# Sliding-window attention beside a gated feed-forward: attention kept transposed, its weights spread through DRAM, the down projection behind the next projections

## The chip, the cores and the metric

One core of a Trainium2 chip runs the kernel. Its engines work side by side, each on its own queue of instructions in order: TensorE (PE: matmuls, with weight loads PEld), VectorE (DVE), ScalarE (ACT), GpSimd (POOL) and SyncE (SP, which here only issues DMAs). Data move between DRAM, the SBUF (128 partitions) and the PSUM banks that TensorE writes. The metric is the time of one execution on the device, in microseconds (us); lower is better.

## The reference

The input is 2048 tokens of width 640 (bf16). A layer norm without learned scale feeds two branches whose sum is added to the input:

```python
def _A_ref(x, wqkv, wo):                 # D = 640, H = 32 heads, Dh = 20
    W, dil = 8, 2
    qkv = (x @ wqkv).reshape(B, S, 3, H, Dh).transpose(2, 0, 3, 1, 4)
    q, k, v = qkv[0], qkv[1], qkv[2]
    idx = pos[:, None] - off[None, :]    # off = 0, 2, ..., 14
    mask = idx >= 0
    ...
    logits = jnp.einsum("bhsd,bhswd->bhsw", q, kg) * scale
    logits = jnp.where(mask[None, None, :, :], logits, -1e9)
    attn = _softmax(logits, axis=-1)
    o = jnp.einsum("bhsw,bhswd->bhsd", attn, vg)
    return o.transpose(0, 2, 1, 3).reshape(B, S, D) @ wo

def _B_ref(x, w_gate, w_up, w_down):     # F = 1536
    return ((x @ w_gate) * (x @ w_up)) @ w_down

xn = _layernorm(x, axis=-1)
return x + _A_ref(xn, A_wqkv, A_wo) + _B_ref(xn, B_w_gate, B_w_up, B_w_down)
```

So each token attends, per head, to eight tokens: itself and those 2, 4, ... 14 positions back.

## The kernel before

**Tiling.** The 2048 tokens are 16 tiles of 128 (index t), grouped into four chunks of 512 (index c). The width 640 is five groups of 128 (KT), the inner width 1536 twelve (FT). `xnT` holds a chunk's normalized input transposed: width on partitions, tokens along the free axis.

**Order.** The kernel does not issue instructions as its loops run. Each piece of work is a `Step` with an engine, a cost, dependencies (`deps`) and an order (`after`); `Plan.order` (L56) simulates the engines, takes at each point the ready step with the least slack, and the instructions are issued in the order that results. `pe_main` (L367) chains PE's steps into a fixed sequence and gives them six PSUM banks in turn (`ring`); only the logits are slipped in between (`urgent`). A step's `margin` is time that the planner adds to a wait. The DMAs on SP are a queue in order too: a DMA that waits holds those behind it.

**Per chunk.** Normalization (`ln`, L334) on DVE for the first eight tiles, on ACT and POOL for the rest; transposes (`transposes`, L379) on PE for chunk 0, by DMA from SP for the others. `qk` (L454) projects q and k transposed: output width on partitions (so that the four partitions jl of a head and the five groups hold its 20 elements), 512 tokens free, five banks each of five matmuls. Their weights are read with a stride of five columns. ACT copies the banks to `q` and `k`; `k` has 14 extra tokens in front (`halo`, L442). `vproj` (L488) projects values the other way: 128 tokens on partitions, two banks of 320 columns a tile; ACT copies them with the heads innermost to `v_t`, and POOL stores them to a DRAM buffer `vD`.

**Attention.** `products` (L559) multiplies q with k shifted by each of the eight offsets, two offsets an instruction, on DVE. `fold` (L538) adds the five groups: in chunks 1 to 3 down to one term, written over the parts of `q` and `k` no longer needed; in chunk 0 only to three (FIRST = 1, LEFT). `logits` (L583) sums over the four partitions of a head with a matrix of ones, `Ek`, on PE: four matmuls side by side, each giving 32 heads on their own 32 partitions; chunk 0 does this once for each of its three terms and lets PSUM add. Half a chunk, n, fills one bank: partition = offset pair and head, free = tokens. The first half's bank gets the mask. ACT copies the bank to `L`, and a DMA transpose on SP turns it to `LT`: tokens on partitions, offsets and heads free. `softmax` (L627) then works on 2 x 8 x 32 values a partition: maximum by three pairwise steps, subtract, exponential on ACT, sum by three steps, reciprocal, scaling to the weights `a`.

**Values.** `load_v8` (L670) loads, for a tile, the eight shifted value rows of each token from `vD`: 1280 KB, three buffers. `av` (L698) multiplies them with the weights (5120 elements a partition), adds the eight offsets in three steps to `o` (tokens on partitions), and a DMA transpose on SP makes `oT`.

**Feed-forward.** `glu` (L742): for each of 12 groups, five matmuls of 512 columns for gate and five for up; ACT copies both banks, DVE multiplies them to `hT`. `down` (L800) adds, for each tile, twelve matmuls with `wd` over `hT` and five with `wo` over `oT` in one bank, in two column halves; ACT copies, and POOL adds the result onto the output in DRAM, which was seeded with the input (`seed`, L783). The last two tiles are added to the input on DVE and stored by SP.

**Sequence on PE.** At the start, tile by tile while input arrives: transposes and values of chunk 0; then q, k of chunk 0 and the fourth tile's values, q, k and values of chunk 1. Then per chunk c: gate and up of c, down of c (with the normalization of chunk c+2 between its tiles, `between`, L914), and q, k, values of c+2. The value weights are loaded first, on ACT's queue; q's and k's follow on SP's, then gate, up, and, behind value loads, down's and the output's.

Of the kernel before, what the change touches and what calls it, by code (L numbers as in the profile page):

```python
# [14 lines left out]
class Step:  # L15


    __slots__ = ("eng", "cost", "deps", "fn", "late", "succ", "idx", "start", "end", "left", "occ", "urgent", "after", "floor", "margin", "kb")

    def __init__(self, eng, cost, fn, deps, occ=None, after=()):  # L20
        self.eng, self.cost, self.fn = eng, cost, fn
        self.after = [d for d in after if d is not None]
        self.deps = [d for d in deps if d is not None] + self.after
        self.occ = cost if occ is None else occ
        self.succ = []
        self.urgent = False
        self.floor = 0.0
        self.margin = 0.0
        self.kb = 0


class Plan:
# [3 lines left out]
    RAW = 0.116  # L36
    INORDER = ("DVE", "PE", "ACT")
# [4 lines left out]
    def add(self, eng, cost, fn, deps=(), occ=None, after=(), kb=0):  # L42
        s = Step(eng, cost, fn, deps, occ, after)
        s.kb = kb
        s.idx = len(self.steps)
        self.steps.append(s)
        return s
# [8 lines left out]
    def order(self):  # L56
# [4 lines left out]
        for s in reversed(self.steps):  # L61
            s.late = min([t.late for t in s.succ], default=0.0) - s.cost
# [45 lines left out]
def kernel(  # L108
# [17 lines left out]
    H = 32  # L126
# [33 lines left out]
    negm = const.tile([P, 2, HALO], F32, name="negm")  # L160
    vD = dram.tile([HALO + S, D], BF, name="vD")
# [28 lines left out]
    WL = {}  # L190

# [5 lines left out]
    def part(n):  # L197
        src = A_wqkv[:, 2 * D + n * NS : 2 * D + (n + 1) * NS].rearrange("(i p) f -> p i f", p=P)
        return lambda: nc.scalar.dma_start(out=wv[:, :, n * NS : (n + 1) * NS], in_=src)
# [8 lines left out]
    def consts0():  # L208
        wz = new("wz", [P, CS], BF, "gs", 5)
        nc.vector.memset(wz[:], 0.0)  # L210
        hold(wv)()
# [10 lines left out]
    def consts_m():  # L222
        nc.gpsimd.memset(negm[:], 0.0)
        for i in range(W):
            w = W - 1 - i
            if w:
                nc.gpsimd.memset(negm[H * (i % 4) : H * (i % 4 + 1), i // 4, 0 : DIL * w], -1e9)

    def consts_z():
        zt = new("zt", [P, D], BF, "v_t", 3)  # L230
        nc.gpsimd.memset(zt[0:HALO, :], 0.0)
        nc.gpsimd.dma_start(out=vD[0:HALO, :], in_=zt[0:HALO, :])

    wo_r = A_wo.rearrange("(h j) d -> j h d", h=H, j=Dh)

    def wo_load():
        for jl in range(JL):
            src = wo_r[jl : jl + 1, :, :]
            src = bass.AP(tensor=src.tensor, offset=src.offset, ap=[[Dh * D, H], [JL * D, KT], [1, D]])
            nc.sync.dma_start(out=wo[jl * H : (jl + 1) * H, :, :], in_=src)  # L240

    C0 = add("POOL", 0.6, consts0)
    WV = [add("ACT", 4.6, part(0), [C0], occ=0.45)]
    WV.append(add("ACT", 5.6, part(1), occ=0.45, after=[WV[0]]))
    X[3] = add("ACT", 5.0, load_x(3, nc.scalar), occ=0.45, after=[WV[1]])
    TB = add("ACT", 1.6, table, after=[X[3]])
    CZ = add("POOL", 3.0, consts_z, [C0], occ=1.2)
# [63 lines left out]

    def ln_mean(t):
# [63 lines left out]
    XDMA = 4  # L376
    GP = {}

    def transposes(t):  # L379
        c, q = divmod(t, CH)  # L380

        def slot():
            if q == 0:
                new(("xnT", c), [P, KT, CS], BF, "xnT", 2)
# [27 lines left out]
        if t < CH:  # L412
# [7 lines left out]
            if t:  # L420
                behind(VE[t - 1][0], TT[t])
# [5 lines left out]
        else:  # L427
            if c == 1:
                a = TT[t] = chain[0] = add("SP", 3.0, dma, [XT[t]], occ=1.28, after=[chain[0]])
            else:  # L430
                a = TT[t] = add("SP", 2.8, dma, [XT[t], GP.get(c - 2)], occ=1.28, kb=200)
# [7 lines left out]
    Q, Kk, LL = {}, {}, {}  # L439
    HALOCP = {}  # L440

    def halo(c):  # L442
        def fn():
            k = new(("k", c), [P, KT, HALO + CS], BF, "k", 2)
            if c == 0:
                nc.vector.memset(k[:, :, 0:HALO], 0.0)
            else:
                nc.scalar.copy(k[:, :, 0:HALO], T["k", c - 1][:, :, CS : CS + HALO])
        if c == 0:
            HALOCP[c] = add("DVE", 0.1, fn)  # L450
        else:
            HALOCP[c] = add("ACT", 0.25, fn, [LL.get(2 * c - 3), *Kk[c - 1]])

    def qk(c, lo, n, rs=(0, 1)):  # L454
        for r in rs:
            for j in range(KT):
                key = ("qk", c, r, j, lo)

                def pe(i0, i1, key=key, r=r, j=j):
                    if i0 == 0:  # L460
                        new(key, [P, 512], F32, "ps", 6, psum)
                    for i in range(i0, i1):
                        nc.tensor.matmul(T[key][:, 0:n], lhsT=(wk if r else wq)[:, i, :].rearrange("p (c b) -> p c b", b=KT)[:, :, j],  # L463
                                         rhs=T["xnT", c][:, i, lo : lo + n], start=(i == 0), stop=(i == KT - 1))

                def ev(key=key, r=r, j=j):
                    if r == 0 and j == 0 and lo == 0:
                        new(("q", c), [P, KT, CS], BF, "q", 2)
                    dst = T["k", c][:, j, HALO + lo : HALO + lo + n] if r else T["q", c][:, j, lo : lo + n]
                    nc.scalar.copy(dst, T[key][:, 0:n])  # L470

                one = n / 2400 + 0.0027
                ts = range(c * CH + lo // P, c * CH + (lo + n) // P)
                mine = [WK if r else WQ, *[TX.get(t, TT[t]) for t in ts], LL.get(2 * c - 3)]
                if c or r or j:
                    a = pe_main(KT * one, lambda pe=pe: pe(0, KT), mine + [TT[t] for t in ts])
                else:
                    pe_main(3 * one, lambda pe=pe: pe(0, 3), mine)
                    a = pe_main(2 * one, lambda pe=pe: pe(3, KT), [TT[t] for t in ts], banks=0)
                e = add("ACT", 0.16 + n / 1200, ev, [a, HALOCP[c]], occ=0.07 + n / 1200)  # L480
                ring.append(e)
                (Kk if r else Q).setdefault(c, []).append(e)

    VS = {}

    VE = {}

    def vproj(t, ns=(0, 1)):  # L488
        c, q = divmod(t, CH)
        evs = VE.setdefault(t, [])  # L490
        for n in ns:
            def pe(i0, i1, n=n):
                if i0 == 0:
                    new(("psv", t, n), [P, 512], F32, "ps", 6, psum)
                for i in range(i0, i1):
                    nc.tensor.matmul(T["psv", t, n][:, 0:NS], lhsT=T["xnT", c][:, i, q * P : (q + 1) * P],  # L496
                                     rhs=wv[:, i, n * NS : (n + 1) * NS], start=(i == 0), stop=(i == KT - 1))

            def ev(n=n):
                if n == 0:  # L500
                    new(("v_t", t), [P, D], BF, "v_t", 3)
                nc.scalar.copy(  # L502
                    T["v_t", t][:].rearrange("p (j h) -> p j h", j=Dh, h=H)[:, :, n * H // 2 : (n + 1) * H // 2],
                    T["psv", t, n][:, 0:NS].rearrange("p (h j) -> p j h", h=H // 2, j=Dh),
                )

            if t < 3 and n == 0:
                pe_main(3 * 0.136, lambda pe=pe: pe(0, 3), [TX[t], WV[n]])
# [476 lines left out]
```

## Time and profile before

| | |
|---|---|
| median of 3 runs | 260.86 us (260.27 to 261.1) |
| the profiled execution | 262.23 us |
| its span, first to last instruction | 260.5 us |
| granted TensorE clock | 1.00 |
| busy, share of span: POOL, ACT | 22%, 51% |
| bytes moved by DMA | 46.54 MB, 179 GB/s |
| value loads, v<-vD | 16 of 1280 KB, 9.3 us to landing (median) |
| value stores, vD<-v_t | 16 of 160 KB, 5.1 us |
| transposes LT, oT, xnT | 8, 16, 12; 3.1, 3.6, 4.0 us |
| gate, up, down weights | 1920 KB each; 8.6, 12.6, 11.0 us |

All durations come from the one profiled execution; the span is what its trace covers, and 1.73 us lie around it. A group line of the profile reads: line of the kernel, engine, operation, output <- inputs, shapes, count | busy us in all, mean ns of one | idle time of the engine just before them and what ended it. A line of the waits reads: who <- for whom: us in total, times, longest. A line of the timeline reads: start, length, engine, line, operation, count, idle before and what ended it. Matmuls are pipelined and their ends are modelled: a single one shows 379 ns at 512 columns while they follow each other faster, so distances between starts are the better measure.

### The profile page before, as it was taken

The page shows a single profiled execution, that of the slowest core. Times are in us where ns is not written, and L with a number is a line of the kernel's source. Part 1 is how long each engine was busy: PE and PEld are TensorE (multiplying, and loading weights), DVE is VectorE, ACT ScalarE, POOL GpSimd, SP SyncE. Part 2 cuts the span into 40 slices and gives each one's busy share as a digit, 9 for nine tenths or more (in the row PEclk, how much of TensorE's full clock was granted, in tenths as well). Part 3 has the DMA queues.
Part 4 walks back from the last instruction along what each step waited for, and adds up shares of the span by engine and source line. Part 5 has one row for each costly group of instructions (what it writes and reads, how often), then busy time and mean ns, then how long its engine had stood idle before and what let it go on. Part 6 is the DMA issues. An engine that isn't in the chain of part 4 may idle for free.

```text
span 260.5 us, 3925 instructions
## 1 busy us (share of the span) xinstructions
PE 253.1 (97%) x1462; PEld 141.1 (54%) x1462; DVE 221.4 (85%) x308; ACT 132.2 (51%) x265; POOL 57.6 (22%) x93
## 2 busy tenths in 40 slices
PE   6999999999997999999999999999999999999895
PEld 2655555444675656544467655644457654445563
DVE  5764998899999968999999959989999887699711
ACT  3755566699821357579951255475531245283100
POOL 4650002054731201107932110200121210000110
PEclk9999999999999999999999999999999999999999
DMA  7999997999999422993339956951136849951341
GB/s 222 340 264 178 397 384 166 337 363 248 200 163 254 49 35 48 366 259 106 127 109 149 247 49 199 337 217 25 25 101 72 227 41 309 184 170 25 49 54 50
DMA packets 51507, 46.54 MB, mean 179 GB/s; under 512 B 24626, under 2 KB 49472, under 8 KB 51424
## 3 DMA queue, kind: packets, MB, share of 16 engines
q1 hardware_dynamic: 46704, 37.10, 53.1%
q0 software_dynamic: 3184, 8.05, 16.2%
q10 hardware_dynamic: 1600, 1.15, 1.4%
q8 instruction: 11, 0.18, 0.3%
q14 instruction: 8, 0.07, 0.1%
HBM read 35.39 MB, written 7.55 MB: 165 GB/s over the span
## 4 chain that ended last, share of the span: by engine, by line
PE 56%; DVE 10%; DMA 6%; issue 1%; ACT 0%; SPq 0%
PE ps L751 20%; PE ps L814 16%; PE ps L463 8%; PE ps L817 7%; DVE v L705 5%; PE ps L496 4%; DMA v<-vD 4%; DMA oT<-o 2%; DVE v L714 2%; DVE hT L767 1%; PE pl L592 1%; DVE v L718 1%; DVE o L723 0%; DVE s L639 0%; DVE d L644 0%
## 5 line engine op out<-in xcount | busy, mean ns | idle before, releaser
L751 PE MATMUL ps<-xnT,wg 128*128 128x512 bf16 x240 | 59.6, 379 | 0.0
L751 PE MATMUL ps<-xnT,wu 128*128 128x512 bf16 x240 | 59.6, 379 | 0.0
L814 PE MATMUL ps<-wd,hT 128*128 128x320 bf16 (+2 forms) x384 | 57.6, 299 | 0.9 <-DVE hT L767 0.9
L705 DVE TENSOR_TENSOR v<-v,a 128x5120 bf16<-128x5120 bf16 x16 | 45.1, 2820 | 2.5 <-DMA v<-vD 2.3
L814 PEld LDWEIGHTS <-hT 128*128 128x128 bf16 x384 | 36.9, 98 | 17.4 <-DVE hT L767 1.4
L573 DVE TENSOR_TENSOR pw<-q,k 128x2560 bf16<-128x2560 bf16 x28 | 41.0, 1486 | 5.4 <-ACT k L470 5.2
L751 PEld LDWEIGHTS <-wu 128*128 128x128 bf16 x240 | 23.5, 98 | 28.3
L751 PEld LDWEIGHTS <-wg 128*128 128x128 bf16 x240 | 23.4, 98 | 27.8 <-issue 0.2
L829 ACT COPY y<-ps 128x320 f32<-128x320 f32 x28 | 11.5, 426 | 51.1 <-PE ps L817 38.4
L756 ACT CAST us<-ps 128x512 bf16<-128x512 f32 x48 | 28.1, 586 | 13.1 <-PE ps L751 11.8
L756 ACT CAST gs<-ps 128x512 bf16<-128x512 f32 x48 | 28.2, 587 | 12.3 <-PE ps L751 12.3
L858 POOL DMA_DIRECT2D out_dram<-y x14 | 12.2, 871 | 82.2 <-ACT y L829 82.2
L817 PE MATMUL ps<-wo,oT 128*128 128x320 bf16 (+2 forms) x160 | 27.0, 299 | 1.5 <-DMA oT<-o 1.5
L544 DVE TENSOR_TENSOR pw<-pw 128x2048 bf16<-128x2048 bf16 (+1 forms) x26 | 24.4, 971 | 0.0
L496 PE MATMUL ps<-wv,xnT 128*128 128x320 bf16 x160 | 23.4, 299 | 0.4 <-ACT xnT L409 0.4
L714 DVE TENSOR_TENSOR v<-v 128x2560 bf16<-128x2560 bf16 x16 | 23.7, 1483 | 0.0
L463 PE MATMUL ps<-xnT,wq 128*128 128x512 bf16 x100 | 22.5, 380 | 0.2 <-DMA xnT<-x 0.2
L463 PE MATMUL ps<-xnT,wk 128*128 128x512 bf16 x100 | 22.3, 379 | 0.0
L517 POOL DMA_DIRECT2D vD<-v_t x16 | 9.0, 563 | 56.9 <-ACT v_t L502 56.9
L767 DVE TENSOR_TENSOR hT<-gs,us 128x512 bf16<-128x512 bf16 x48 | 19.4, 415 | 0.7 <-ACT us L756 0.7
L817 PEld LDWEIGHTS <-oT 128*128 128x128 bf16 x160 | 15.4, 98 | 8.0 <-DMA oT<-o 1.8
L496 PEld LDWEIGHTS <-xnT 128*128 128x128 bf16 x160 | 15.1, 98 | 7.7 <-issue 1.1
(71 smaller groups left out, 233.1 us busy)
## 6 DMA issues: line engine op xcount, KB each, us to landing
v<-vD SPq DMA_DIRECT2D x16, 1280.0 KB, 9.3
vD<-v_t POOLq DMA_DIRECT2D x16, 160.0 KB, 5.1
out_dram<-y POOLq DMA_DIRECT2D x14, 160.0 KB, 3.8
out_dram<-in_A_x_dram POOLq DMA_DIRECT2D x3, 640.0 KB, 4.3
wg<-in_B_w_gate_dram SPq DMA_DIRECT2D x1, 1920.0 KB, 8.6
wu<-in_B_w_up_dram SPq DMA_DIRECT2D x1, 1920.0 KB, 12.6
wd<-in_B_w_down_dram SPq DMA_DIRECT2D x1, 1920.0 KB, 11.0
x<-in_A_x_dram SPq DMA_DIRECT2D x11, 160.0 KB, 4.9
```

The lines of the kernel that those rows point to most:

```text
L463: nc.tensor.matmul(T[key][:, 0:n], lhsT=(wk if r else wq)[:, i, :].rearrange("p (c b) -> p c b", b=KT)[:, :, j], rhs=T["xnT", c][:, i, lo ...
L496: nc.tensor.matmul(T["psv", t, n][:, 0:NS], lhsT=T["xnT", c][:, i, q * P : (q + 1) * P], rhs=wv[:, i, n * NS : (n + 1) * NS], start=(i == ...
L544: nc.vector.tensor_tensor(w[:, :, lo:hi, :], w[:, :, lo:hi, :], w[:, :, a:b, :], ALU.add)
L573: nc.vector.tensor_tensor(o, qh, kh, ALU.mult)
L705: nc.vector.tensor_tensor(v[:].rearrange("p w (j h) -> p w j h", j=Dh, h=H), v[:].rearrange("p w (j h) -> p w j h", j=Dh, h=H), T["a", n][ ...
L714: nc.vector.tensor_tensor(v[:, 0:4, :], v[:, 0:4, :], v[:, 4:8, :], ALU.add)
L751: nc.tensor.matmul(ps[:], lhsT=(wu if r else wg)[:, i, f * P : (f + 1) * P], rhs=T["xnT", c][:, i, :], start=(i == 0), stop=(i == KT - 1))
L756: nc.scalar.copy(s[:], T[key][:])
L767: nc.vector.tensor_tensor(h[:], T["gs", c, f][:], T["us", c, f][:], ALU.mult)
L814: nc.tensor.matmul(ps, lhsT=T["hT", c, f][:, q * P : (q + 1) * P], rhs=wd[:, f, sl], start=(f == 0), stop=(f == FT - 1 and not wo_part))
L817: nc.tensor.matmul(ps, lhsT=T["oT", t][:, g, :], rhs=wo[:, g, sl], start=False, stop=(g == KT - 1 and f1 == FT))
L858: nc.gpsimd.dma_start(out=out_flat[t * P : (t + 1) * P, :], in_=T["y", t][:], accum_op=ALU.add)
```

## The change

**Values** are projected like q and k (`proj`, three times per chunk, and `project`): transposed, into a tile `v` with 14 extra tokens in front, two buffers. The DRAM buffer `vD`, the value stores, the eight-fold loads, `L`, `LT` and their transposes are gone. At the start it is now q that is projected tile by tile (`proj_tile`: 128-column matmuls, five output groups in two banks); its weights come first, on ACT's queue, split by rows, and those of k and v follow on SP's.

**Logits and softmax.** Chunk 0 folds to one term as well (FIRST = 3), so each half takes one pass. A bank now holds all eight offsets and 64 tokens on the free axis; the partition is the head and which quarter of the half's 256 tokens (E = 64). Eight matmuls of 256 columns fill it. `softmax` works on the bank itself: two reductions (`top`, `total`) take the place of the six pairwise steps; `d`, `m`, `s` and `a` have one buffer.

**Weights.** `store` writes the half's weights `a` to DRAM (128 KB), and `spread` loads them back with each head's row repeated on its four partitions (512 KB). `av` multiplies shifted windows of `v` with them, two instructions a tile, and adds the offsets; the last step writes `oT` itself, so its transpose is gone. `wo` is loaded in one DMA with partitions in the projections' order.

**Order.** After gate and up of chunk c, PE does q, k and values of chunk c+2 and then down of chunk c. `xnT` has three buffers. The normalization on ACT is held by the steps in LN_HOLD. The planner multiplies DVE costs by 1.03, and the logits' margin is 3 us instead of 4.

The diff, cut to its core:

```diff
+    PACE = {"DVE": 1.03, "ACT": 1.0}
...
+    LN_HOLD = ((2,1,0),(2,1,2),(2,1,4),(0,0),(0,11),(2,2,0),(2,2,1),(2,2,2))
...
-            a = GL[t] = add("ACT", 0.95, ln_mean(t), [X[t], HT.get((t // CH - 2, t % CH + 2))], occ=0.87)
+            a = GL[t] = add("ACT", 0.95, ln_mean(t), [X[t], held(LN_HOLD[t - 2 * CH])], occ=0.87)
...
+    EARLY = True
+    XB = 3 if EARLY else 2
...
+    def proj_tile(r, t, ns=(0, 1)):
+        for n in ns:
+            j0, j1 = ((0, 3), (3, KT))[n]
+            def pe(i0, i1, n=n, j0=j0, j1=j1):
+                for j in range(j0, j1):
                     for i in range(i0, i1):
+                        nc.tensor.matmul(T["psv", r, t, n][:, (j - j0) * P : (j - j0 + 1) * P], lhsT=lhs(r, i, j),
+                                         rhs=T["xnT", c][:, i, q * P : (q + 1) * P], start=(i == 0 and j == j0), stop=(i == KT - 1),
...
+    def proj(c, r, lo=0, n=CS):
+        for j in range(KT):
+            def pe(key=key, j=j):
+                for i in range(KT):
+                    nc.tensor.matmul(T[key][:, 0:n], lhsT=lhs(r, i, j),
+                                     rhs=T["xnT", c][:, i, lo : lo + n], start=(i == 0), stop=(i == KT - 1))
+            old = LL.get(2 * c - 3) if r < 2 else O16.get(CH * (c - 1) - 1)
...
+                for b in range(2):
+                    for j in range(4):
+                        nc.tensor.matmul(l[H * j : H * (j + 1), 4 * b : 4 * b + 4, :], lhsT=Ek[:],
+                                         rhs=parts[b][i][:, :, E * j : E * (j + 1)],
...
+        def top():
+            m = new(("m", n), [P, E], F32, "m", 1)
+            nc.vector.tensor_reduce(m[:], T["lps", n][:].rearrange("p w s -> p s w"), AX.X, ALU.max)
         def sub():
+            d = new(("d", n), [P, W, E], F32, "d", 1)
+            nc.vector.tensor_tensor(d[:], T["lps", n][:], T["m", n][:, None, :].to_broadcast([P, W, E]), ALU.subtract)
...
+        def total():
+            s = new(("s", n), [P, E], F32, "s", 1)
+            nc.vector.tensor_reduce(s[:], T["d", n][:].rearrange("p w s -> p s w"), AX.X, ALU.add)
...
+        def store():
+            aD = new(("aD", n), [H, 4, W * E], BF, "aD", 2, dram)
+            nc.sync.dma_start(out=aD[:].rearrange("h e f -> e h f"), in_=T["a", n][:].rearrange("p w s -> p (w s)"))
+        def spread():
+            ae = new(("aE", n), [P, 4, W, E], BF, "aE", 2)
+            src = bass.AP(tensor=src.tensor, offset=src.offset, ap=[[4 * W * E, H], [0, JL], [1, 4 * W * E]])
+            nc.sync.dma_start(out=ae[:], in_=src)
+        AS[n] = add("SP", 2.4, store, [AA[n], AE.get(n - 2)], occ=0.5, kb=128)
+        AE[n] = add("SP", 3.5, spread, [AS[n], AM.get(2 * n - 3)], occ=0.5, kb=512)
...
+        def mul(b):
+                o = T["av", t][:, :, :, b * E : (b + 1) * E]
+                w = bass.AP(tensor=w.tensor, offset=w.offset, ap=[list(w.ap[0]), [E, W], [0, KT], [1, E]])
+                v = T["v", c][:, :, q * P + b * E : q * P + b * E + E]
+                v = bass.AP(tensor=v.tensor, offset=v.offset, ap=[list(v.ap[0]), [DIL, W], *[list(x) for x in v.ap[1:]]])
+                nc.vector.tensor_tensor(o, v, w, ALU.mult)
...
-        between(c + 2, lambda q: down(c * CH + q))
-        if c + 2 < NCH:
-            halo(c + 2)
-            qk(c + 2, 0, CS)
+            if c + 2 < NCH:
+                for t in range((c + 2) * CH, (c + 3) * CH):
+                    ln(t)
+                    transposes(t)
+                project(c + 2)
             for q in range(CH):
-                vproj((c + 2) * CH + q)
+                down(c * CH + q)
```

More of the change, by code (lines that the diff above doesn't have):

```diff
@@ L447, in fn @@
             else:
-                nc.scalar.copy(k[:, :, 0:HALO], T["k", c - 1][:, :, CS : CS + HALO])
+                nc.scalar.copy(k[:, :, 0:HALO], T[PROJ[r], c - 1][:, :, CS : CS + HALO])
         if c == 0:
-            HALOCP[c] = add("DVE", 0.1, fn)
+            HALOCP[r, c] = add("POOL", 0.3, fn, after=[RS[0]])
         else:
[L452 to L461, printed above, removed]
-                    for i in range(i0, i1):
[L463 to L508, printed above, removed]
-                a = pe_main(2 * 0.136, lambda pe=pe: pe(3, KT), [TT[t]], banks=0)
-            else:
-                a = pe_main(KT * 0.136, lambda pe=pe: pe(0, KT), [TT[t], TX.get(t), WV[n]])
-            e = add("ACT", 0.425, ev, [a, VS.get(t - 3), CZ], occ=0.35)
```

320 lines of the change are left out of this document (153 added, 167 removed).

## The prediction

> **What bounds the kernel now.** First the page's busy shares, then TensorE (PE) in order of time, then who waited for whom on VectorE (DVE), last the groups by shape for prices.
>
> ```profile
> span 260.5 us, 3925 instructions
> PE 253.1 (97%) x1462; PEld 141.1 (54%) x1462; DVE 221.4 (85%) x308; ACT 132.2 (51%) x265; POOL 57.6 (22%) x93
> PE 56%; DVE 10%; DMA 6%; issue 1%; ACT 0%; SPq 0%
> ```
>
> A busy PE need not be PE at its rate, so I check it: the chain of waits has the gate and up matmuls of chunk 1 as 120 in 25.90 us, 0.216 each for 512 columns, and the 320-column ones as 12 in 1.63, 0.136 each. At these rates the timeline has PE back to back nearly from 6.54 us to the last matmul. The places where it is not are these (start, length, what; a length includes the modelled end of the last matmul, so I use counts times the rates):
>
> ```profile
> 22.36 1.52 PE L496 MATMUL ps<-wv,xnT 128*128 128x320 bf16 x10
> 24.10 5.59 PE L463 MATMUL ps<-xnT,wq 128*128 128x512 bf16 x25 [0.22 <-DMA xnT<-x]
> ...
> 77.23 1.79 PE L814 MATMUL ps<-wd,hT 128*128 128x320 bf16 x12
> 80.50 0.85 PE L817 MATMUL ps<-wo,oT 128*128 128x320 bf16 x5 [1.47 <-DMA oT<-o]
> ...
> 241.26 0.84 PE L817 MATMUL ps<-wo,oT 128*128 128x320 bf16 x5
> 242.56 0.31 PE L814 MATMUL ps<-wd,hT 128*128 128x320 bf16 x1 [0.45 <-DVE hT L767]
> 243.30 2.21 PE L814 MATMUL ps<-wd,hT 128*128 128x320 bf16 x15 [0.43 <-DVE hT L767]
> ```
>
> The gaps: 24.10 - (22.36 + 1.36) = 0.38 us (the transposed chunk 1 is late), 80.50 - (77.23 + 1.63) = 1.64 (the attention output's transpose is late for the down projection), 242.56 - (241.26 + 0.68) = 0.62 and 243.30 - (242.56 + 0.14) = 0.60 (the last products of gate and up). Together 3.24 us. PE is the bound and there is little to take from it; DVE at 85% is close behind.
>
> ```profile
> DVE m L639 <- DMA LT<-L: 7.6, 6, 1.9
> DVE pw L573 <- ACT k L470: 5.2, 1, 5.2
> DVE s L639 <- ACT d L652: 3.3, 3, 1.9
> DVE v L705 <- DMA v<-vD: 2.3, 1, 2.3
> ```
>
> These are totals, times, longest. DVE starts attention at 23.18 (after the 5.2 us wait for k) and ends it at 246.03, 222.85 us; in them it waits 7.6 + 3.3 + 2.3 + 0.7 (for up) = 13.9, so it has 208.9 us of work.
>
> ```profile
> L705 DVE TENSOR_TENSOR v<-v,a 128x5120 bf16<-128x5120 bf16 x16 | 45.1, 2820 | 2.5 <-DMA v<-vD 2.3
> L573 DVE TENSOR_TENSOR pw<-q,k 128x2560 bf16<-128x2560 bf16 x28 | 41.0, 1486 | 5.4 <-ACT k L470 5.2
> L814 PEld LDWEIGHTS <-hT 128*128 128x128 bf16 x384 | 36.9, 98 | 17.4 <-DVE hT L767 1.4 <-issue 0.5
> L463 PEld LDWEIGHTS <-wq 128*128 128x128 bf16 x100 | 11.6, 118 | 9.8 <-DMA xnT<-x 0.5 <-issue 0.2
> ```
>
> **The change on PE.** Values: 160 matmuls of 320 columns (21.8 us) become 25 of 512 per chunk, 5.4 per chunk: nothing. In chunk 0 the part done tile by tile while inputs arrive is now q, in 128-column matmuls, a new weight for each: 100 of them. The nearest row is the last tile's 12 matmuls of 128 columns in 0.67 us in the chain, 0.056 each, 5.6 against 40 x 0.136 = 5.4 for values before: +0.2. But q's weights are read with a stride of five columns and such a load takes 118 ns, not 98. Bounds: 0.056 (load hidden) and 0.118 (nothing overlaps), +0.2 to +6.4. I take 0.058, +0.4, since 98 ns loads already run at a 0.056 spacing, so a load's length isn't its spacing. The first 0.38 of a delay here is free: chunk 1 waits for its transpose anyway. So 0 on the path.
>
> The Trainium skill (TensorE: Matmul & The Clock Gate, Back-to-back issue gap) says that a stream of load and matmul pairs at 128 columns runs at about 81 ns a pair. The trace's 0.67/12 = 56 ns disagrees, for packed weights; by the page the sum would be some 2.3 us higher. This is the first rival.
>
> Logits: chunk 0 had three rounds of four concurrent 512-column matmuls per half (37.05 to 37.82, 0.77 us), the others one round (0.33), so a round is 0.22 and the fixed part 0.11. Now each half is two rounds of 256 columns. If a round is half as long: 0.33, two halves save 0.87 in all. If a round's four weight loads set it, 0.22 stays: 0.55, chunk 0 saves 0.44 and six halves lose 1.3: +0.9. I take the middle, 0.
>
> Down of chunk 0 moves behind the 16.2 us of q, k, v of chunk 2 (3 x 25 x 0.216), from 68 to about 84 us. The outputs it waited for until 80.5 are ready long before (below), and they are written by DVE itself, without the 3.6 us transpose. The 1.64 us gap goes. What is late next there: project of chunk 2 at 68 needs the chunk's normalized, transposed input some 20 us earlier than before (88.1). That work now starts at the value evictions of chunk 1 (about 35 us), where ScalarE (ACT) is 5.9 of 10 busy from 40 to 50; four tiles cost 4 x (0.74 + 0.19 + 0.84 + 0.20 + 0.93) = 11.6 us of ACT beside 24 evictions of 0.59; in the trace the same mix fitted 50 to 70 us without a PE stall. A third buffer takes away the wait for the old chunk. Without that cover, each microsecond late is one on PE.
>
> The 1.22 us at the end: DVE must hand over the last products earlier. I count 0.8 of them. Sum on PE: -1.64 - 0.8 + 0 + 0 = -2.4 us.
>
> **On DVE.** Removed per half chunk, by the groups' means: maximum tree 0.290 + 0.221 + 0.187, sum tree 0.420 + 0.287 + 0.225, 1.63 in all. Added: two reductions of 512 f32 values, not in the trace. Below, the 256-pair level, 0.420; nearest, a 512-element f32 pass, 0.69; above, twice that, 1.38 (logits' bank, strided). 16 x r - 13.0: -6.3, -2.0, +9.1; I take -2.0. Subtraction, reciprocal and scaling keep their size (subtract now reads the bank itself; 0.69 kept). Weighting the values: 2 x 1.486 for 2.820, the products being the same size, type and kind: 16 x 0.152 = +2.4. Chunk 0's sums now fold to one term on DVE: 8 x 0.686 = +5.5. Together +5.9: 214.8 us of work. It starts earlier: q is ready 1.4 us after values were, k 5.4 later, so about 19.3 instead of 23.2. Without waits DVE ends at 234.1; with all 13.9 of the old waits at 248.0. The last output is needed about 255.5 - 2.4 = 253 (the last tile's wo matmuls stand at 255.54). So DVE may idle 19 us before the end moves, which covers the +5.9; without cover it would be +5.9.
>
> The output of the last half is not late either way, but the products of gate and up are in the same line, so I keep 0.4 of the end gaps.
>
> **DMA and the queues.** Gone: 16 loads of 1280 KB (9.3 us median, 6.1 to 15.6), 17 stores, 16 output transposes, 8 logit transposes (1.19 us of SP's queue each, 3.1 to landing, the 7.6 us of DVE waits). New per half: a store of 128 KB, then, after it lands, a load of 512 KB, both on SP in order. Behind a waiting store stand the transposes for chunk c+2 and further loads. A small store at the end (160 KB) landed in 1.8 us; loads of 160 KB took 2.3 to 8.4. So the trip is 4 to some 17 us; I take 6 (store 2, load 4). DVE has the second half's products (about 10 us with folds) or two tiles of the half before (2 x 5.4) in that time.
> Values of chunk 2 overwrite those of chunk 0, so ACT's evictions at 78 wait until DVE has finished the fourth tile: 19.3 + 21 (products, folds) + 2 x 3.3 + 4 x 5.4 + 12 x 0.34 = 72.6 us. Behind a blocked ACT stand PE's banks: five groups fit, so PE stops only from about 84. That allows 11 us of slip.
> ACT loses the logits' copies (4.7 us) and gains three halo copies (0.8); POOL loses the 9.0 us of value stores. Neither sets the end. The planner's factor of 1.03 on DVE and its logits margin of 3 us for 4 change the order only: a logits group placed 1 us earlier holds PE if the folds are late, and so far PE waits for none.
>
> **Sum.** The profiled execution took 262.23 us with 1.73 around its span; the runs' median is 260.86, 1.4 lower. 260.5 - 2.4 gives a span of 258.1; taken off the median, 258.5.
>
> **Rivals.**
> 1. *q's strided weights set the pace.* If the 20 ns by which they are longer all shows, 0.076 a matmul, 7.6 us for 5.4: +2.2 - 0.38 = +1.8, giving 260.2; this is no measurable change. For: 118 against 98. Against: at 512 columns the strided ones run at 0.216 like the packed.
> By the page named above it would be 100 x 0.081 = 8.1, +2.3, so 260.7.
> 2. *The trip through DRAM (slower).* Place: between scaling and the first weighting of each half, on SP's in-order queue. In chunk 0 the new load stands behind gate, up, down and out weights, 6.6 MB at the 380 GB/s of those slices, 17 us from 21.9. If a trip takes 12 us against 8.5 of cover, 8 x 3.5 = 28 us of DVE idle; DVE ends at 262 instead of 253, +9 on the span of 258.1: about 267 for the median. It decides from 19/8 = 2.4 us of exposed wait per half. For: value loads took up to 15.6. Against: these were 2.5 times larger and 20 MB of them leave the queues.
> A packet takes 47 ns here (53.1% of 16 engines' span over 46,704); should the store's 128 packets fall to four engines, 32 each instead of 8 add 1.1 us to every trip, which is in its chance.
> The Trainium skill (DMA: Bandwidth & Descriptors, Rules for kernel authors) says that an outermost dimension under 16 confines a DMA to that many engines, and the store's DRAM side starts with 4; no run so far shows it.
> 3. *The change doesn't do what it says:* the weighting loses DVE's double rate. Slope of the f32 rows, 0.268 us per 256 elements: 2.83 for 2560, 32 x 1.34 = +43 us, DVE end 277, some 282. Against: the products row has the same broadcasts.
> 4. *Gaps only move:* logits at +0.9, the end gaps kept at 1.22, chunk 2's input 1 us late: -1.64 + 0.9 + 1 = +0.3, 261.1.
>
> **Chances.** Forecast 0.58 (256.5 to 260.0); rival 1 0.08; rival 4 0.12, two thirds of it no change, the rest slower as more inputs are late; rival 2 0.15; rival 3 0.03; the rest, 0.04, slower. A run of this kernel can tell 0.3% (0.8 us) from no change, so faster is under 260.1. Faster 0.58; no change 0.08 + 0.08 = 0.16; slower 0.26. Low end: all gaps and 0.87 of logits, -4.1, 256.7, less 0.3 of spread; high end 263.2, between rivals 4 and 2, leaves out some 0.17. The likeliest alone: 256.4 to 260.0.
>
> **What would show it.** Right: no wait of PE for the output before its wo matmuls; q of chunk 0 as 100 matmuls spaced 0.056 to 0.06; products from about 19 us; reductions near 0.69, weighting near 1.49; DVE waits for the spread weights under 10 us in all; down of chunk 0 from about 84. Wrong: PE gaps at q of chunk 2, DVE waits over 2.4 us per half on the load, logits over 0.5 us a half.

## The result and the profile after

The changed kernel takes 272.34 us (272.2 to 272.68), the kernel before, beside it, 260.98: a ratio of 1.0417, 95% interval 1.0369 to 1.0466. It is 11 us slower, where 258.5 had been forecast and 263.2 was the end of the range. The profiled execution took 272.2 us with a span of 270.5, 10.0 more than before, at a granted clock of 1.00. All medians here are over every execution; e4 and e13 below each had one in a slower state of the chip, without which their medians are 259.61 and 268.31.

The page of the changed kernel, its busy shares and its chain of waits:

```profile
span 270.5 us, 3849 instructions
PE 253.6 (94%) x1493; PEld 140.0 (52%) x1493; DVE 228.4 (84%) x299; ACT 127.3 (47%) x251; POOL 50.7 (19%) x77
DVE 46%; PE 23%; DMA 22%; POOL 4%; issue 2%; ACT 1%; SPq 0%; ACTq 0%; DVEq 0%; POOLq 0%
```

TensorE's busy time is the same as before (253.1), VectorE's 7 us more. The chain has turned round: TensorE held 56% of it, now VectorE holds 46% and DMA 22%. TensorE's work didn't grow; it is held up. The waits of the changed kernel (who <- for whom: us in total, times, longest):

```profile
DVE av L681 <- DMA aE<-aD: 15.9, 7, 5.7
PE ps L780 <- DVE hT L731: 6.1, 5, 2.7
DVE s L635 <- ACT d L628: 5.0, 1, 5.0
PE pl L587 <- DVE k L541: 3.3, 2, 1.7
PE ps L714 <- ACT us L719: 1.6, 1, 1.6
```

VectorE idles 15.9 us for the spread weights and 5.0 for one exponential, and TensorE waits for VectorE: for the products of gate and up (`hT`) and for the folded logits (`k`), or for a copy on ScalarE (`us`) that itself stands behind VectorE. With counts times the rates of before, TensorE's gaps from 100 us on are 2.26 and 2.33 (logits' folds), 1.74 (ScalarE's copy), 2.91 and 0.54 (`hT` of chunk 2) and 3.66 (`hT` of chunk 3): 13.4 against 3.24 before. That is the 10 us.

The prices, from the groups by shape (count | busy us, mean ns | idle before):

```profile
L681 DVE TENSOR_TENSOR av<-v,aE 128x2560 bf16<-128x2560 bf16 x32 | 46.9, 1486 | 15.9 <-DMA aE<-aD 15.9
L635 DVE TENSOR_REDUCE s<-d 128x64 f32<-128x512 f32 x8 | 8.3, 1038 | 5.1 <-ACT d L628 5.0
L615 DVE TENSOR_REDUCE m<-pl 128x64 f32<-128x512 f32 x8 | 5.5, 686 | 0.0
```

The weighting costs what was taken, the maximum (of the bank in PSUM) too; the sum, which reads SBUF, costs 1.04 us where 0.69 was taken.

And the end of the span, where it is decided. First VectorE's timeline, then TensorE's (start, length, what, idle before):

```profile
250.84 0.42 DVE L731 TENSOR_TENSOR hT<-gs,us 128x512 bf16<-128x512 bf16 x1
251.18 1.48 DVE L681 TENSOR_TENSOR av<-v,aE 128x2560 bf16<-128x2560 bf16 x1
252.58 0.42 DVE L731 TENSOR_TENSOR hT<-gs,us 128x512 bf16<-128x512 bf16 x1
252.91 2.35 DVE L691 TENSOR_TENSOR av<-av 128x2560 bf16<-128x2560 bf16 x2
255.29 0.49 DVE L689 TENSOR_TENSOR oT<-av 128x640 bf16<-128x640 bf16 x1
```

```profile
246.58 0.31 PE L780 MATMUL ps<-wd,hT 128*128 128x320 bf16 x1 [0.16 <-DVE hT L731]
248.32 0.31 PE L780 MATMUL ps<-wd,hT 128*128 128x320 bf16 x1 [1.43 <-DVE hT L731]
...
253.06 2.21 PE L780 MATMUL ps<-wd,hT 128*128 128x320 bf16 x15 [1.43 <-DVE hT L731]
```

The last product of gate and up ends at 252.58 + 0.42 = 253.00 and TensorE goes on at 253.06. The last attention output comes 2.8 us later, long before TensorE wants it. So the deadline on VectorE's queue is the last product, and nearly all of attention stands ahead of it in that queue. The balance against the kernel before shows what moved it. There the last product ended at 243.24. VectorE now starts 23.18 - 19.70 = 3.5 earlier, has 215.0 - 208.9 = 6.1 more work (work is what its time from start to last output leaves after the waits), loses the 13.9 of old waits and gains 21.1 of new ones (15.9, 5.0 and 0.2 for ScalarE's copies): 253.0.

### The profile page after: what moved, and what is told of

Its sections match the earlier page's. It is cut to its first block, busy times and chain, and to the rows that moved or that the text cites. A ratio compares the mean times of both kernels' runs of the same rounds, so it can differ in the third digit from the quotient of the medians.

```text
span 270.5 us, 3849 instructions
## 1 busy us (share of the span) xinstructions
PE 253.6 (94%) x1493; PEld 140.0 (52%) x1493; DVE 228.4 (84%) x299; ACT 127.3 (47%) x251; POOL 50.7 (19%) x77
## 3 DMA queue, kind: packets, MB, share of 16 engines
q0 software_dynamic: 2384, 5.41, 12.2%
## 4 chain that ended last, share of the span: by engine, by line
DVE 46%; PE 23%; DMA 22%; POOL 4%; issue 2%; ACT 1%; SPq 0%; ACTq 0%; DVEq 0%; POOLq 0%
DMA aE<-aD 11%; DVE av L681 11%; PE ps L502 10%; DMA aD<-a 9%; DVE av L691 8%; DVE pw L565 7%; DVE pw L536 5%; PE ps L714 5%; PE ps L780 4%; DVE hT L731 4%; POOL ve L325 3%; DVE s L635 3%; PE ps L476 2%; DVE a L642 2%; PE ps L783 2%
## 5 line engine op out<-in xcount | busy, mean ns | idle before, releaser
L780 PE MATMUL ps<-wd,hT 128*128 128x320 bf16 (+2 forms) x384 | 58.3, 300 | 6.1 <-DVE hT L731 6.1
L681 DVE TENSOR_TENSOR av<-v,aE 128x2560 bf16<-128x2560 bf16 x32 | 46.9, 1486 | 15.9 <-DMA aE<-aD 15.9
L565 DVE TENSOR_TENSOR pw<-q,k 128x2560 bf16<-128x2560 bf16 x28 | 40.3, 1486 | 1.0 <-ACT k L506 1.0
L691 DVE TENSOR_TENSOR av<-av 128x2560 bf16<-128x2560 bf16 (+1 forms) x32 | 36.9, 1154 | 0.2
L824 POOL DMA_DIRECT2D out_dram<-y x14 | 12.2, 874 | 99.9 <-ACT y L795 96.7
L536 DVE TENSOR_TENSOR pw<-pw 128x2048 bf16<-128x2048 bf16 (+1 forms) x28 | 25.4, 952 | 0.0
L502 PE MATMUL ps<-xnT,wv 128*128 128x512 bf16 x100 | 22.4, 380 | 0.0
L325 POOL TENSOR_SCALAR ve<-ss 128x1 f32<-128x1 f32 x8 | 12.6, 1580 | 47.1 <-ACT sq L319 37.1
L731 DVE TENSOR_TENSOR hT<-gs,us 128x512 bf16<-128x512 bf16 x48 | 20.1, 419 | 0.2 <-ACT us L719 0.2
L502 PEld LDWEIGHTS <-wv 128*128 128x128 bf16 x100 | 11.7, 118 | 9.8
L502 PE MATMUL ps<-xnT,wq 128*128 128x512 bf16 x75 | 16.7, 379 | 0.0
```

The lines of the kernel that those rows point to most:

```text
L325: nc.gpsimd.tensor_scalar(ve[:], T["ss", t][:], scalar1=1.0 / D, scalar2=EPS, op0=ALU.mult, op1=ALU.add)
L502: nc.tensor.matmul(T[key][:, 0:n], lhsT=lhs(r, i, j), rhs=T["xnT", c][:, i, lo : lo + n], start=(i == 0), stop=(i == KT - 1))
L536: nc.vector.tensor_tensor(w[:, :, lo:hi, :], w[:, :, lo:hi, :], w[:, :, a:b, :], ALU.add)
L565: nc.vector.tensor_tensor(o, qh, kh, ALU.mult)
L681: nc.vector.tensor_tensor(o, v, w, ALU.mult)
L691: nc.vector.tensor_tensor(v[:, 0:k], v[:, 0:k], v[:, k : 2 * k], ALU.add)
```

## The experiments

Two theories fit these lines. **The trip**: the way of the weights through DRAM, 7.1 to 9.2 us from the store's issue to the landing of the load, leaves VectorE idle, and its lateness reaches TensorE (rival 2 of the prediction). **The order**: down behind the projections puts work where it collides. Each run is the changed kernel with the edit shown, and no other. The table has all thirteen, by the last product of gate and up in the profiled execution (its end, and what of the span lies behind it):

| kernel | weights, exponential: VectorE's idle us | last product | span | behind it | median us | ratio to before, 95% |
|---|---|---|---|---|---|---|
| the change | 15.9, 5.0 | 253.00 | 270.5 | 17.5 | 272.34 | 1.0369 to 1.0466 |
| e1 no trip | 0, 5.7 | 237.66 | 257.6 | 19.9 | 259.65 | 0.9937 to 0.9977 |
| e2 chunk 0 folds to three | 19.6, 0 | 250.20 | 270.4 | 20.2 | 270.45 | 1.0310 to 1.0417 |
| e3 normalization early | 14.8, 0 | 246.49 | 264.1 | 17.6 | 265.39 | 1.0085 to 1.0231 |
| e4 old order | 12.4, 0 | 241.59 | 259.1 | 17.5 | 260.06 | 0.9939 to 1.0009 |
| e5 old order, costs | 7.2, 0 | 238.61 | 257.3 | 18.7 | 259.03 | 0.9911 to 0.9965 |
| e6 old order, no trip | 0, 1.9 | 237.01 | 257.4 | 20.4 | 259.05 | 0.9909 to 0.9959 |
| e7 tiny reductions | 16.1, 5.0 | 255.48 | 273.0 | 17.5 | 273.19 | 1.0415 to 1.0539 |
| e8 store over 128 rows | 4.0, 5.0 | 240.32 | 257.8 | 17.5 | 260.18 | 0.9959 to 1.0017 |
| e9 quarter loads alone | 7.6, 5.0 | 244.33 | 261.8 | 17.5 | 264.14 | 1.0092 to 1.0157 |
| e10 = e8 and e3 | 2.6, 0.5 | 236.97 | 257.1 | 20.1 | 258.77 | 0.9897 to 0.9936 |
| e11 = e8, old order | 2.4, 1.4 | 236.96 | 257.4 | 20.4 | 259.11 | 0.9905 to 0.9944 |
| e12 costs | 8.8, 5.0 | 246.12 | 263.8 | 17.7 | 264.96 | 1.0122 to 1.0178 |
| e13 reductions between | 17.5, 0 | 251.72 | 269.2 | 17.5 | 269.60 | 1.0205 to 1.0323 |

Wherever VectorE is late, 17.5 to 17.7 us of the span lie behind its last product: TensorE's remaining work. Where 18.7 to 20.4 lie behind it, TensorE runs without a stop and the time is 258.8 to 259.7. e2 is the one exception: TensorE's clock in its profiled execution was 0.95 behind 250 us, which lengthened that part; with the clock at 1.00 it took 269.21.

**e1: the trip left out**; `aC` is a constant tile of 0.125.

```diff
+        nc.gpsimd.memset(aC[:], 0.125)
...
-            nc.sync.dma_start(out=aD[:].rearrange("h e f -> e h f"), in_=T["a", n][:].rearrange("p w s -> p (w s)"))
+            pass
...
-            nc.sync.dma_start(out=ae[:], in_=src)
+            T["aE", n] = aC
```

> The weights' store to DRAM and load back are left out; the weighting multiplies with a constant tile (0.125), so the attention's result isn't the reference's. The planner's steps and the order on every engine stay as in the changed kernel. Theory A (DVE is the bound, and the trip's 15.9 us of DVE waits move its end nearly one for one): DVE ends at about 241 instead of 255.8, PE's gaps fall from 13.5 to under 5 us, time 260 to 263. Rival B (POOL and ACT being blocked around 85 to 100 us and the order on PE are the cause): under 3 us less, above 269. Rival C (DVE's added work alone): 268 or more.

259.65 us, a little under what theory A gave: with no trip the new order loses nothing, though the 5.0 us wait for the exponential is still there. The trip is needed for the loss, and VectorE's added work alone does not make it.

**e2: chunk 0 folded to three terms again**, which takes 5.5 us from VectorE.

```diff
-    FIRST = 3
+    FIRST = 1
```

> Only chunk 0's folding is undone: three terms are left to PE's PSUM sums as before the change, 5.5 us less on DVE, 0.9 us more on PE. Theory A, DVE the bound for work as for waits: 267 to 269. If DVE's work is hidden in its waits for the trip: 271.5 to 273. Theory B gives the latter.

270.45: only 1.9 us better, 3.1 at clock 1.00, and in neither range. The 5.0 us wait for the exponential went with the 5.5 us of work, and the waits for the weights grew from 15.9 to 19.6; the last output comes 6 us earlier. But the last products stand behind the last output here, so that the last of them is only 2.8 us earlier, and the time follows the product.

**e3: the normalization of tiles 13 to 15 earlier**, in the new order.

```diff
-    LN_HOLD = ((2,1,0),(2,1,2),(2,1,4),(0,0),(0,11),(2,2,0),(2,2,1),(2,2,2))
+    LN_HOLD = ((2,1,0),(2,1,2),(2,1,4),(0,0),(0,11),(0,11),(0,11),(0,11))
```

> Only the hold of the normalization of tiles 13 to 15 on ACT is moved to that of tile 12 (product 11 of chunk 0), some 10 us earlier, so that POOL's small steps fall between DVE's dependent steps and not beside the back-to-back products at 85 to 92 us. Theory B (a POOL step of 7.4 us held by DVE, which holds ACT, the exponential and DVE's sum for 5.0 us): that wait is gone, 267 to 269. Theory A with the trip alone: 271.5 to 273; DVE then waits for the load instead.

265.39 (262.15 to 265.82), 7 us better and more than expected. The 5.0 us wait for the exponential is gone, and with it 1.1 of the weights' waits. Where it came from in the changed kernel, in the timelines of GpSimd, VectorE and ScalarE, one fence each:

```profile
85.14 7.39 POOL L325 TENSOR_SCALAR ve<-ss 128x1 f32<-128x1 f32 x1 [9.75 <-DVE k L541]
```

```profile
85.65 5.69 DVE L565 TENSOR_TENSOR pw<-q,k 128x2560 bf16<-128x2560 bf16 x4
91.26 1.22 DVE L536 TENSOR_TENSOR pw<-pw 128x2048 bf16<-128x2048 bf16 x1
92.39 0.69 DVE L615 TENSOR_REDUCE m<-pl 128x64 f32<-128x512 f32 x1
...
100.52 1.05 DVE L635 TENSOR_REDUCE s<-d 128x64 f32<-128x512 f32 x1 [4.98 <-ACT d L628]
```

```profile
97.11 2.54 ACT L355 ACTIVATE x<-x,ns,rstd 128x640 bf16<-128x640 bf16 x3 [6.11 <-POOL ns L348]
99.86 0.63 ACT L628 ACTIVATE d<-d 128x512 f32<-128x512 f32 x1
```

A step of 128x1 values on GpSimd takes 7.39 us, from 85.14 until VectorE comes from its products to the reduction at 92.39. With the normalization ScalarE waits 6.11 us for it and the GpSimd steps behind it, the exponential stands behind that, and VectorE waits for the exponential.

**e4: the old order**, down of chunk c ahead of the projections of c+2; everything else as changed.

```diff
-    EARLY = True
+    EARLY = False
```

> Only the order on PE is undone: down of chunk c before q, k, v of chunk c+2, two buffers for the transposed input, normalization between the down tiles. Theory A: order isn't the cause, 270 to 275 (the output may be late for down of chunk 0 again, some 2 us). Rival D (the order itself costs the 11 us): 261 to 265.

260.06, no measurable change from before. The new attention costs nothing by itself; the loss appears with the order. The weights' waits are still 12.4 us here, and the wait for the exponential is gone. But on VectorE the last product ends 7.0 us ahead of the last output (248.56), 4.2 us more than in the new order, and the last product is what counts.

**e5: e4's old order, and the trip's measured times as the planner's costs**; **e12: the same costs in the new order.**

```diff
-        AS[n] = add("SP", 2.4, store, [AA[n], AE.get(n - 2)], occ=0.5, kb=128)
-        AE[n] = add("SP", 3.5, spread, [AS[n], AM.get(2 * n - 3)], occ=0.5, kb=512)
+        AS[n] = add("SP", 4.3, store, [AA[n], AE.get(n - 2)], occ=0.5, kb=128)
+        AE[n] = add("SP", 5.0, spread, [AS[n], AM.get(2 * n - 3)], occ=0.5, kb=512)
```

> The old order of down and the projections, and the planner told the trip's measured times (store 4.3 us for 2.4, load 5.0 for 3.5). If the exposed trip is a matter of placing, VectorE's waits for the spread weights fall from 12.4 us to under 6; TensorE had only some 2 us of gaps left in the old order, so the time falls by at most that, to 258.3 to 260.1. If the waits cannot be placed elsewhere they stay at 10 us or more and the time at 260 or above.

> The new order and the change's own trip; only the planner is told the trip's measured times (4.3 us for 2.4, 5.0 for 3.5). If the loss comes from an order of instructions made for a shorter trip, other work is put into the wait, VectorE's waits for the weights fall from 15.9 us to under 8, and the time to 261 to 267. If the trip's length itself is what costs, because VectorE has nothing else to do at these places, the waits stay over 12 us and the time at 270 to 273.

e5: 259.03 with 7.2 us of waits, at the floor (the waits were expected to fall under 6). e12: 264.96; the waits fall from 15.9 to 8.8 (expected under 8), the exponential's 5.0 stays. So 7 of the 11 us came from the order of VectorE's instructions, with the trip as it was. What the edit changes is less than its expectation says: for a step with `kb`, a DMA's size, the planner's simulation replaces the cost by 2.0 us + kb/340 (L97 to L99), so that the trip still lands after 5.9 us in it. The new costs only enter the slack, and work that leads to a trip is taken earlier.

**e6: the old order without the trip** (e1's and e4's edits).

> The old order, and the trip left out (the weights' store and load are not issued, a constant tile stands in for the spread weights, so the output is not the reference's). If the order was what let the trip hurt, the trip is worth little here: 258 to 259.6, 0.5 to 2 us under the old order with the trip. If the trip costs the same wherever down stands, some 12 us as in the new order, the time falls to about 248 to 250; TensorE's 253 us of work at full rate speaks against that.

259.05, 1.0 us under e4 and the same as e5: in the old order the trip costs 1 us, and with e5's costs nothing that shows. This is TensorE's floor in either order, as e1 and e10 show with 259.65 and 258.77.

**e8: the store over 128 rows; e9: its quarter loads alone.** e8 lays the scratch in DRAM out by quarters and heads, so that the store's outermost dimension is 128 and no longer 4; the spread has then to be four loads. e9 keeps the old layout with four loads. The cut is e8's; e9 has its second part, with the old layout's offsets.

```diff
-            aD = new(("aD", n), [H, 4, W * E], BF, "aD", 2, dram)
-            nc.sync.dma_start(out=aD[:].rearrange("h e f -> e h f"), in_=T["a", n][:].rearrange("p w s -> p (w s)"))
+            aD = new(("aD", n), [4, H, W * E], BF, "aD", 2, dram)
+            nc.sync.dma_start(out=aD[:].rearrange("e h f -> (e h) f"), in_=T["a", n][:].rearrange("p w s -> p (w s)"))
...
-            nc.sync.dma_start(out=ae[:], in_=src)
+            for e in range(4):
+                nc.sync.dma_start(out=ae[:, e], in_=bass.AP(tensor=src.tensor, offset=src.offset + e * H * W * E, ap=[[W * E, H], [0, JL], [1, W * E]]))
```

> The new order; the scratch in DRAM is laid out so that the store's outermost dimension is 128 rows instead of 4, and the spread is four loads of 128 KB, one for each quarter, instead of one of 512 KB. If the store's 4 leading rows confine it to few engines, the store takes 1.8 to 2.6 us from issue to landing instead of 3.2 to 4.3, the trip 6 to 7.5 instead of 7.2 to 9.4, VectorE's waits for the weights 15.9 us go to 7 to 12 and the time to 268 to 271. If the store's time is a fixed latency it stays at 3 us or more, and with three more issues on the queue the time is 271.5 to 274.

> The new order; the store as in the change (4 leading rows), but the spread is four loads of 128 KB, one for each quarter. It takes the run with 128 rows apart: if the store's shape was what brought the 12 us, the store stays at 3.2 to 4.3 us, VectorE's waits for the weights at 12 us or more, and the time at 269 to 273. If the gain came from the first quarter being there earlier than the whole half, the waits fall under 7 us and the time to 260 to 264.

e8: 260.18, 12 us better than the change, and more than either theory of its expectation allowed. e9: 264.14 with 7.6 us of waits, far from its first theory and just outside its second: the quarter loads bring two thirds of the gain, the layout one third. The store's time reads from SP's timeline, from the store's issue to the spread's, which waits for it. Of the change:

```profile
159.41 0.54 SPq L648 DMA_DIRECT2D aD<-a  x1
162.64 0.54 SPq L654 DMA_DIRECT2D aE<-aD  x1
176.72 0.55 SPq L648 DMA_DIRECT2D aD<-a  x1
180.01 0.54 SPq L654 DMA_DIRECT2D aE<-aD  x1
```

and of e8:

```profile
168.73 0.33 SPq L648 DMA_DIRECT2D aD<-a  x1
170.47 2.46 SPq L654 DMA_DIRECT2D aE<-aD  x4
...
223.92 0.33 SPq L648 DMA_DIRECT2D aD<-a  x1
225.63 2.45 SPq L654 DMA_DIRECT2D aE<-aD  x4
```

The four quickest of the change's eight stores take 3.2 to 3.4 us (the others 4.2 to 4.3; in e9 the four quickest take 3.3), the three quickest of e8's 1.7 (the others 2.2 to 4.8, beside other transfers). The page of e8 gives a quarter load 2.6 us to landing against 4.1 for the whole and 3.1 for e9's quarters, so the layout shortened the loads as well. The first weighting needs the first two quarters only:

```profile
aE<-aD SPq DMA_DIRECT2D x32, 128.0 KB, 2.6
```

From the change to e9 the waits fall by 8.3 us and the time by 8.2; from e9 to e8 by 3.6 and 4.0. The waits in the change were seven, of 0.96 to 5.71 us and five of them under 2, so 1.5 us off the store and as much off the first quarter removes most of them. The 4.98 us wait stayed in e8 and costs little there, as e10 shows.

The Trainium skill (DMA: Bandwidth & Descriptors, Rules for kernel authors) says that an outermost dimension under 16 confines a DMA to at most that many engines; the trace agrees in the direction, since the same 128 KB take 3.2 us with 4 rows and 1.7 with 128 in the quickest stores, but how many engines moved them no run here shows.

**e10: e8 with the early normalization of e3; e11: e8 in the old order.**

> The new order, the store over 128 rows with four quarter loads, and the normalization of tiles 13 to 15 held as early as in the run where it alone was moved (265.4). If what counts is the sum of VectorE's idle time, the 4.98 us wait for the exponential, still there with 128 rows, goes, and the time falls from 260.2 to the floor that the runs without a trip show, 259 to 259.7. If the earlier normalization cost something of its own, which the late products (5.8 us of waits) of that run suggest, the time is 261 to 263.

> The old order of down and the projections, the store over 128 rows with four quarter loads. If the order matters only through VectorE's slack, the short trip makes both orders equal within the measurement: 258.7 to 259.7 here, as without the trip (259.05). If the new order has a cost of its own, the old one is more than 1 us better than 260.2.

258.77 and 259.11. With a short trip both orders are at the floor. e10 is 1.4 us under e8, so that much is the most that the exponential's wait cost there. e10 is the fastest kernel here, 0.9916 of the one before (0.9897 to 0.9936), and its chain of waits is TensorE's:

```profile
PE 96%; DVE 1%; DMA 1%; issue 1%; ACT 0%
```

**e7 and e13: what holds GpSimd.** One instruction with one input is put behind VectorE's products: in e7 a tiny one behind each of chunk 1, in e13 a whole one behind each of its second half.

```diff
                 nc.vector.tensor_tensor(o, qh, kh, ALU.mult)
+                if c == 1:                                            # e7
+                    nc.vector.tensor_reduce(zz[0:H], negm[0:H, 0, 0:8], AX.X, ALU.max)
...
+                if c == 1 and hf == 1:                                # e13
+                    nc.vector.tensor_reduce(zz[:], wk[:, 0, 0:512], AX.X, ALU.max)
```

> The new order; behind each of the eight product instructions of chunk 1 VectorE does one tiny reduction (32x8 to 32x1, some 0.1 us, 0.8 us in all), which computes nothing that is used. If VectorE's run of independent two-input products keeps GpSimd out, GpSimd's 128x1 step of 7.39 us falls under 2.5 us, the 4.98 us wait for the exponential goes, and the time falls to 264 to 268, where moving that normalization earlier brought it (265.4). If the step is long for another reason it stays near 7 us and the time is 272 to 274.

> The new order and the change's own trip; behind each of the four product instructions of the second half of chunk 1 VectorE reduces 128x512 values to 128x1, some 0.6 us each, 2.4 us in all, which nothing uses. It is the wider form of the tiny reductions that did not free GpSimd. If a whole instruction with one input is what GpSimd needs, its 128x1 step of 7.39 us ends behind the first of them, under 4 us, the 4.98 us wait for the exponential shrinks to under 2, and the time is 269 to 272. If only the step of VectorE that reads PSUM frees it, the step grows to 9 us or more and the time to 273 to 276.

e7 missed: GpSimd's step took 8.96 us and the time was 273.19. The tiny reductions took 0.14 us, but the next product started 0.07 us after they had, so the products followed each other at 1.47 us instead of 1.40, still without a pause. e7's executions ran at clocks of 0.98 to 0.99, so its 0.9 us over the change are not read as a loss. In e13 it went as expected: 269.60, 2.7 us better (267.05 to 271.06, so that the size is loose) with 2.4 us more work on VectorE, and the wait for the exponential was gone. GpSimd's timeline in e13, then VectorE's:

```profile
85.01 2.01 POOL L326 TENSOR_SCALAR ve<-ss 128x1 f32<-128x1 f32 x1 [9.79 <-DVE k L542]
87.11 0.55 POOL L328 TENSOR_TENSOR rstd<-ve,mhalf 128x1 f32<-128x1 f32 x1
87.74 1.28 POOL L326 TENSOR_SCALAR ve<-ss 128x1 f32<-128x1 f32 x1
```

```profile
85.49 1.49 DVE L566 TENSOR_TENSOR pw<-q,k 128x2560 bf16<-128x2560 bf16 x1
86.89 0.68 DVE L568 TENSOR_REDUCE zz<-wk 128x1 f32<-128x512 bf16 x1
87.48 1.48 DVE L566 TENSOR_TENSOR pw<-q,k 128x2560 bf16<-128x2560 bf16 x1
88.88 0.68 DVE L568 TENSOR_REDUCE zz<-wk 128x1 f32<-128x512 bf16 x1
```

The two `ve` steps end at 87.02 and 89.02, 0.13 and 0.14 us into a reduction. The products with two inputs, back to back, keep GpSimd out, and a whole one-input instruction lets it in. No run here changes only the number of inputs, so that the second input is the reason is not shown.

## Why the prediction was wrong

**The step that failed** is the deadline: "The last output is needed about 255.5 - 2.4 = 253 ... So DVE may idle 19 us before the end moves". VectorE's last duty for TensorE is not the last output but the last product of gate and up, which stands among the weighting of the last tiles. The lines shown before had it: TensorE reaches the last two groups at 241.26 + 0.68 = 241.94 and waits there 0.45 and 0.43 for `hT`. With the prediction's own numbers, VectorE's end without waits, 234.1, less the 2.8 us behind the last product is 231.3; TensorE, without the 1.64 gap, is there at 240.3: room for 9.0 us of idling, not 19. The prediction saw these products in the same queue, and priced them at 0.4 us of end gaps.

The runs give this figure. e8 idles 9.0 us and hands over at 239.90 + 0.42 = 240.32, as TensorE gets there. VectorE's timeline in e8, then TensorE's:

```profile
239.90 0.42 DVE L731 TENSOR_TENSOR hT<-gs,us 128x512 bf16<-128x512 bf16 x1
```

```profile
239.37 0.84 PE L783 MATMUL ps<-wo,oT 128*128 128x320 bf16 x5
240.05 2.53 PE L780 MATMUL ps<-wd,hT 128*128 128x320 bf16 x16
242.42 0.84 PE L783 MATMUL ps<-wo,oT 128*128 128x320 bf16 x5
```

The sixteen matmuls take 242.42 - 240.05 = 2.37 us where their rate gives 2.18: a wait of 0.2. The change idles 20.9 and is 12.2 us slower than e8, nearly one for one. The idle time was the other half of it: with under 10 us, as the prediction's signs had it for the weights, the nearer deadline would have cost 1 us at most. The 1.22 us of gaps at the end, of which 0.8 were counted as a gain, were this deadline already reached.

**Rival 2** had place and mechanism: the trip, on SP's queue, with VectorE idle 2.3 us per wait. Its point of decision, 19/8 = 2.4 us a half, came from the same 19 us; with 9 it is 1.1, and the measured 15.9/8 = 2.0 lies between the two. Its 267 with a chance of 0.15 was too low on both. The trip was taken as 6 us (store 2, load 4) and is 7.1 to 9.2 (store 3.2 to 4.3, load 3.7 to 5.0). The confined store was priced at 1.1 us a trip; the wide one saved 1.5.

**Not in any rival**: the 5.0 us at the exponential. The prediction looked for the moved normalization's cover on ScalarE for chunk 2, where it held (no gap of TensorE between 68 and 84 us), but not at chunk 3's, which now stands beside VectorE's products and goes through GpSimd.

**What held.** VectorE's work: 214.8 forecast, 215.0 measured, though the eight sums took 0.35 us more each, 2.8 in all, so other terms were as much too high; to that extent the agreement is luck. Its start: 19.3, measured 19.70. q of chunk 0: 25 matmuls from 9.74 to 11.19 us, 0.058 each, as taken, so the stride of the weights cost nothing (rival 1 falls; its 260.2 and 260.7 are 260.3 and 260.8 by its own terms). Weighting: 1.486 (rival 3 falls). Logits: 0.33 to 0.34 us a half where nothing held them, the lower end, where the middle was taken. The wait for the attention output, 1.64, is gone. These are TensorE's side of the sum, and e10 shows it: 258.77, where 258.5 was forecast for a kernel in which VectorE keeps up.

**The order** was costed at nothing on VectorE. It cost room there: the change has 2.8 us behind its last product, the old order 7.0, 3.5 us less of waits for the weights and none of the 5.0 for the exponential. Why the planner places them so was not taken apart.

## What to carry to other kernels

An engine's slack ends at the first thing that the bounding engine waits for in its queue, not at its last output: read the deadline from the waits of the bounding engine, however short they are, and count what stands behind that instruction, not ahead of it. A planner that orders by slack has to be told what a new round trip really costs: seven of the eleven microseconds came back from two corrected costs, with the trip itself unchanged. A scratch buffer's layout is free to choose: putting 128 rows outermost and loading what is needed first in pieces of its own brought the whole loss back.

## What the runs showed of the hardware

- A 128 KB store whose DRAM side leads with 4 rows took 3.2 to 3.4 us from its issue to that of the load waiting for it, in the four quickest of eight; with 128 rows 1.7, in the three quickest. Its issue on SP took 0.54 to 0.55 and 0.33 us in these.
- GpSimd's step of 128x1 values waited through 7.39 us of VectorE's products and folds, five instructions with two inputs in a row, and got in during a reduction of 0.69 us (in e13 of 0.68), but not beside reductions of 32x8 values that took 0.14. The Trainium skill (SBUF — State Buffer, Who interferes with whom) says that an instruction of VectorE with two inputs in SBUF contends with a GpSimd instruction that reads SBUF. The trace agrees on the exclusion; the end of one such instruction was not enough here, where the next followed without a pause.
- The reduction of 512 f32 values took 0.69 us from PSUM and 1.04 from SBUF, with the same pattern of access. The first takes the maximum and the second the sum, so whether the source or the operation makes the difference stays open.
